# Attention and two mixtures on one core: the first mixture's second product regrouped around what follows it

## The chip, the core and the metric

The kernel runs on one core of a Trainium2 chip. Time is device microseconds (us) of one execution; lower is better. PE (TensorE) multiplies matrices, PEld is its weight loading, DVE (VectorE), ACT (ScalarE) and POOL (GpSimd) work elementwise, and SP (SyncE) issues the DMAs. Each engine works through its own instructions in order and waits for the others by semaphores.

## The reference

Masked attention gives x (2304 tokens by 512). The first mixture multiplies it by `w_in`, bends it, and multiplies by `w_out`; the second reads that result in two places only, in the logits and in the slot inputs.

```
h = x @ w_in                                   # 2304 x 2048
g = where(h >= 1, h, where(h <= -1, 0, (h + 1)**2 / 4))
x2 = g @ w_out                                 # 2304 x 512
logits = x2 @ phi                              # phi: 512 x 32
d = softmax(logits, axis=0)                    # over tokens (dispatch)
slot_input = d.T @ x2                          # 32 x 512, 4 slots for each of 8 experts
slot_out[e] = relu(slot_input[e] @ w1[e]) @ w2[e]
c = softmax(logits, axis=1)                    # over slots (combine)
out = c @ slot_out
```

`w_in` and `w_out` arrive as 64-bit floats and are turned into 32-bit ones on the chip.

## The kernel before

**Attention.** 16 pairs of heads go through a pipeline whose order is written out in `PLAN`. Its steps `xh` and `xl` write x, transposed, as two parts (`xt`): ACT copies the rounded high part out of PSUM, DVE subtracts it to get the low one. In some pairs the plan also prepares a half of a weight tile (`w0` to `w2`): the first `READY` = 4 of 32 tiles are made there.

**Weights.** A tile is 128 by 512 values. `w_raw` loads it by SP (512 KB), `w_mul` scales on ACT, `w_bits` does four DVE operations on the bits (L353 to L356), and `w_parts` makes the high and low part: a copy (ACT in the later part) and two POOL operations (L365, L366). Tiles of `w_in` and `w_out` alternate, and the steps of the last 28 are scattered through the main loop (`prep`).

**Main loop.** The tokens are four blocks of 512 and one of 256 (`BLK`); the hidden features are 16 tiles f of 128. A unit is one block and one f, and `VISITS` sets the order of the 80 units, block after block in turns. `h_unit` makes h with 12 matmuls (4 parts of the inner dimension by three products of high and low parts, L423); ACT, DVE, DVE, ACT and POOL then make g as a high and a low part (L430 to L437). Two units later `out_unit` multiplies: 128 tokens by 512 columns, three matmuls each (L453 to L455), kept in PSUM over a visit and added by DVE into `x2p` at its end (L465).

**Behind the loop.** When a block has all its f, `prework` transposes x2 (L555), multiplies by phi (L564), takes exponentials with a running maximum, and sums x2 by them into S (L600); its steps are let in between matmuls after so many rows (`PACE`). `merge` and `last` do the joining of the four row groups and the 256 tokens, with dummy matmuls (`fill`) in their gaps. The last of it, `p_slots` (L743), writes the slot inputs `st`; `tail` runs the experts on them (L845, L873) and the output. The expert weights, 72 pieces of up to 512 KB, are loaded by `feed` into buffers of 4 KB per partition (pools b4 and c4), as these come free.

PSUM has three pools: ptr (three tiles, for h and small things), psc (two double tiles), ppv (one).

Of the kernel before, what the change touches and what calls it, by code (L numbers as in the profile page):

```python
# [14 lines left out]
P = 128  # L15
# [21 lines left out]
class Pair:  # L37
# [172 lines left out]

    def xl(self, a):
        for hi, lo, src in self.xparts(a):
            self.nc.vector.tensor_tensor(out=lo, in0=src, in1=hi.bitcast(F32), op=ALU.subtract)
# [18 lines left out]
READY = 4  # L232


def attention(e, tc, nb=4, wl=(1, 1 + 2 * READY)):
# [36 lines left out]
    for i, u in fill + plan[len(fill):]:  # L272
        if u[0] != "w":
            pairs[i].step(u)
        else:
# [3 lines left out]
            elif u == "w1":  # L279
                e.moe.w_mul(t, c)  # L280
                for fn in e.moe.w_bits(t, c):
                    fn()
            elif u == "w2":
                for fn in e.moe.w_parts(t, c=c, eng=e.ENG["w"]):
                    fn()


class Moe:


    VISITS = [(0, 0, 2), (1, 0, 2), (2, 0, 3), (3, 0, 4),
# [15 lines left out]


    def b4(self, shape, dt, name):
        return self.e.b4.tile(shape, dt, tag="b4", name=name)  # L310

    def c4(self, shape, dt, name):
        return self.e.c4.tile(shape, dt, tag="c4", name=name)

    def make_xt(self):
        for i in range(4):
            for kk in range(4):
                self.xt[i, kk] = self.b4([P, 2, 512], F32R, f"xt{i}{kk}")
        for u in range(2):
            t = self.b4([P, 2, 2, 256], F32R, f"xt4{u}")  # L320
            for a in range(2):
                self.xt[4, 2 * u + a] = t[:, a]

        def xslice(kk, t):
            i, o = t // 512, t % 512
            x = self.xt[i, kk]
            return (lambda w: x[:, 0, o:o + w]), (lambda w: x[:, 1, o:o + w]), self.BLK[i][1] - o
        self.e.xslice = xslice

# [3 lines left out]
    def w_raw(self, i):  # L333
        e, nc = self.e, self.nc
        f = i // 2
        raw = self.b4([P, 512, 2], U32, f"raw{i}")
        nc.sync.dma_start(raw.rearrange("p c t -> p (c t)"), e.w_out[f * P:(f + 1) * P, :] if i % 2 else e.w_in[f])
        self.wt[i] = raw

    def w_mul(self, i, c=slice(0, 512)):  # L340
        if c.start == 0:
            raw = self.wt[i]
            AB = (self.b4 if i < READY else self.c4)([P, 2, 512], F32, f"wab{i}")
# [4 lines left out]
    def w_bits(self, i, c=slice(0, 512)):  # L348
# [3 lines left out]
        return [  # L352
            lambda: v.tensor_scalar(out=Bu, in0=hi, scalar1=0x80000000, scalar2=None, op0=ALU.bitwise_and),  # L353
            lambda: v.scalar_tensor_tensor(out=Au, in0=Au, scalar=3, in1=Bu, op0=ALU.logical_shift_left, op1=ALU.bitwise_or),  # L354
            lambda: v.tensor_scalar(out=Bu, in0=Au, scalar1=0xff800000, scalar2=None, op0=ALU.bitwise_and),
            lambda: v.scalar_tensor_tensor(out=B, in0=lo, scalar=2.0 ** -52, in1=B, op0=ALU.mult, op1=ALU.mult)]  # L356

    def w_parts(self, i, late=False, c=slice(0, 512), eng="A"):
        p = self.nc.gpsimd
        if c.start == 0:  # L360
# [698 lines left out]
```

## Time and profile before

| | us |
|---|---|
| median of 2 runs | 648.97 (648.87 to 649.07) |
| the profiled execution | 649.23 |
| its span, first to last instruction | 647.4 |
| first h matmul | 174.85 |
| last x matmul gives way to the closing chain | 591.36 |
| first expert matmul | 600.09 |

The profiled execution lies 0.26 us above the median; 1.83 us of its time lie outside the span. The three places of the last rows part it into attention, main loop, closing chain and tail.

### The profile page before, as it was taken

The page shows a single profiled execution, that of the slowest core. Times are in us where ns is not written, and L with a number is a line of the kernel's source. Part 1 is how long each engine was busy: PE and PEld are TensorE (multiplying, and loading weights), DVE is VectorE, ACT ScalarE, POOL GpSimd, SP SyncE. Part 2 cuts the span into 40 slices and gives each one's busy share as a digit, 9 for nine tenths or more (in the row PEclk, how much of TensorE's full clock was granted, in tenths as well). Part 3 has the DMA queues.
Part 4 walks back from the last instruction along what each step waited for, and adds up shares of the span by engine and source line. Part 5 has one row for each costly group of instructions (what it writes and reads, how often), then busy time and mean ns, then how long its engine had stood idle before and what let it go on. Part 6 is the DMA issues. An engine that isn't in the chain of part 4 may idle for free.

```text
span 647.4 us, 11524 instructions
## 1 busy us (share of the span) xinstructions
PE 631.3 (98%) x4351; PEld 499.8 (77%) x4351; DVE 402.7 (62%) x721; ACT 311.1 (48%) x756; POOL 301.4 (47%) x339
## 2 busy tenths in 40 slices
PE   7899999999999999999999999999999999999996
PEld 6777778778788888888888888888888878776355
DVE  6899987877367578756677656647533333444233
ACT  5799999999443444433433333323322232334123
POOL 5798886766235457455465544425622221211000
PEclk8799999999999999999999999999999999999999
DMA  4534324332400031110011120000321344449897
GB/s 130 150 101 143 102 83 116 98 87 60 153 1 32 33 132 65 66 65 1 32 66 66 65 66 33 33 14 33 117 98 66 130 147 147 150 167 340 328 382 293
DMA packets 36086, 71.05 MB, mean 110 GB/s; under 512 B 8000, under 2 KB 17344, under 8 KB 36032
## 3 DMA queue, kind: packets, MB, share of 16 engines
q1 hardware_dynamic: 36032, 70.33, 32.0%
q8 instruction: 34, 0.56, 0.4%
q14 instruction: 20, 0.16, 0.1%
HBM read 64.55 MB, written 4.72 MB: 107 GB/s over the span
## 4 chain that ended last, share of the span: by engine, by line
PE 81%; DVE 9%; ACT 4%; issue 1%; POOL 1%; DVEq 0%; ACTq 0%
PE h L423 28%; PE x L453 10%; PE x L455 10%; PE x L454 10%; PE sc L120 4%; PE om L184 3%; PE eh L845 2%; PE acc L873 2%; DVE nm L142 2%; ACT pr L147 2%; PE ps_1p L166 2%; PE sc L113 1%; PE x2t L555 1%; PE om L189 1%; PE ps_0p L166 1%
## 5 line engine op out<-in xcount | busy, mean ns | idle before, releaser
L423 PE MATMUL h<-xt,w 128*128 128x512 f32 (+1 forms) x960 | 212.6, 369 | 0.0
L437 POOL TENSOR_TENSOR g<-ga,g 128x512 fp32r<-128x512 f32 (+1 forms) x80 | 98.6, 1232 | 226.5 <-ACT g L436 197.2
L423 PEld LDWEIGHTS h<-xt,w 128*128 128x128 f32 x960 | 168.5, 188 | 32.5 <-issue 1.8
L432 DVE SCALAR_TENSOR_TENSOR ga<-ga 128x512 f32<-128x512 f32 (+1 forms) x80 | 70.0, 875 | 148.9 <-ACT ga L430 148.8
L453 PE MATMUL x<-w,g 128*128 128x512 f32 x288 | 115.0, 399 | 1.5 <-ACT x2p L241 0.7
L436 ACT CAST g<-ga 128x512 fp32r<-128x512 f32 (+1 forms) x80 | 46.3, 579 | 139.3 <-DVE ga L434 139.3
L454 PE MATMUL x<-w,g 128*128 128x512 f32 x288 | 112.3, 390 | 0.0
L455 PE MATMUL x<-w,g 128*128 128x512 f32 x288 | 112.3, 390 | 0.0
L430 ACT ACTIVATE ga<-h,half 128x512 f32<-128x512 f32 (+1 forms) x80 | 51.6, 645 | 107.2 <-PE h L423 100.5
L158 POOL TENSOR_SCALAR pr<-pr,sm 128x384 f32<-128x384 f32 (+2 forms) x144 | 85.4, 613 | 24.4 <-ACT Q L89 11.4
L147 ACT ACTIVATE pr<-sc,nm 128x512 f32<-128x512 f32 (+2 forms) x144 | 78.6, 559 | 6.4 <-DVE nm L140 3.8
L453 PEld LDWEIGHTS x<-w,g 128*128 128x128 f32 x288 | 54.1, 188 | 16.9 <-issue 3.6
L455 PEld LDWEIGHTS x<-w,g 128*128 128x128 f32 x288 | 54.1, 188 | 11.5
L454 PEld LDWEIGHTS x<-w,g 128*128 128x128 f32 x288 | 54.2, 188 | 9.8
L142 DVE TENSOR_REDUCE nm<-sc 128x2 f32<-128x1024 f32 (+1 forms) x64 | 52.3, 818 | 5.4 <-PE sc L123 4.0
L434 DVE TENSOR_TENSOR ga<-h,ga 128x512 f32<-128x512 f32 (+1 forms) x80 | 50.7, 634 | 1.9
L120 PE MATMUL sc<-K,Q 64*128 64x512 f32 (+3 forms) x384 | 47.7, 364 | 2.7 <-ACT pr L147 2.7
L365 POOL TENSOR_TENSOR wab<-wab,w 128x512 f32<-128x512 f32 (+1 forms) x36 | 44.6, 1238 | 11.6 <-ACT w L241 6.8
L366 POOL TENSOR_TENSOR w<-wab 128x512 fp32r<-128x512 f32 (+1 forms) x36 | 44.5, 1237 | 1.9
L120 PEld LDWEIGHTS sc<-K,Q 64*128 64x128 f32 x384 | 30.5, 198 | 12.3 <-ACT pr L147 4.9
L465 DVE TENSOR_TENSOR x2p<-x,x2p 128x1024 f32<-128x1024 f32 (+1 forms) x32 | 36.8, 1181 | 0.6 <-PE x L455 0.4
L354 DVE SCALAR_TENSOR_TENSOR wab<-wab 128x512 uint32<-128x512 uint32 (+1 forms) x36 | 32.4, 901 | 1.4
(202 smaller groups left out, 774.2 us busy)
## 6 DMA issues: line engine op xcount, KB each, us to landing
ew<-in_w_dram SPq DMA_DIRECT2D x32, 512.0 KB, 4.5
raw<-in_w_in_dram SPq DMA_DIRECT2D x16, 512.0 KB, 3.3
raw<-in_w_out_dram SPq DMA_DIRECT2D x16, 512.0 KB, 3.3
ew<-in_w2a_dram SPq DMA_DIRECT2D x16, 510.0 KB, 6.6
ew<-in_w2b_dram SPq DMA_DIRECT2D x16, 344.0 KB, 6.9
kn<-in_k_dram SPq DMA_DIRECT2D x16, 288.0 KB, 3.7
qn<-in_q_dram SPq DMA_DIRECT2D x16, 288.0 KB, 3.2
vn<-in_v_dram SPq DMA_DIRECT2D x16, 256.0 KB, 3.2
```

Source lines behind the costliest of these rows:

```text
L120: nc.tensor.matmul(sc[:, h, 0:n], self.Q[r, qa, 128 * i:128 * i + 128], self.K[r, ka, 0:n], start=(k == 0), stop=False)
L142: nc.vector.tensor_reduce(out=self.negm[:, 2 * i:2 * i + 2], in_=self.scs[i][:, :, 0:128 * (i + 1)], axis=AX.X, op=ALU.max, negate=True)
L147: self.nc.scalar.activation(pr, sc, AF.Exp, bias=self.negm[:, b:b + 1], accum_out=self.sums[:, b:b + 1])
L158: self.nc.gpsimd.tensor_scalar(out=pr, in0=pr, scalar1=self.sums[:, b:b + 1], scalar2=1.0, op0=ALU.mult, op1=ALU.mult)
L423: nc.tensor.matmul(ph[:, 0:n], w[:, wi, kk], x[:, xi, 0:n], start=(m == 0), stop=(m == 11))
L430: nc.scalar.activation(ga, ph, AF.Relu, bias=e.half[:, 0:1], scale=0.5)
L432: nc.vector.scalar_tensor_tensor(out=ga, in0=ga, scalar=1.0, in1=ga, op0=ALU.min, op1=ALU.mult)
L434: nc.vector.tensor_tensor(out=ga, in0=ph, in1=ga, op=ALU.max)
L437: nc.gpsimd.tensor_tensor(out=gl, in0=ga, in1=gh.bitcast(F32), op=ALU.subtract)
L453: nc.tensor.matmul(px, gh[:, c], w[:, 0], start=first, stop=False)
L454: nc.tensor.matmul(px, gh[:, c], w[:, 1], start=False, stop=False)
L455: nc.tensor.matmul(px, gl[:, c], w[:, 0], start=False, stop=last)
```

## The change

x2 is no longer formed. The logits are g times (`w_out` times phi), and the slot inputs are (dispatch sums of g) times `w_out`. In parts:

- `w_out` tiles are made by one POOL addition, stored to DRAM (`wod`) by SP, and loaded again as `wo` in units 42 to 49. `wo_turn` transposes them, `wo_phi` multiplies by phi, `wo_back` turns the product into `w2p` (128 by 32 for each f).
- All `w_in` tiles come first (i below 16), then `w_out`. `READY` is 6. The unit order is plainly block 0 with all 16 f, block 1, and so on; one tile is prepared in each of the units 0 to 25, as `run` writes it out.
- g is one 32-bit tile, written by DVE at L520. `act_unit` uses three ACT operations and one DVE operation in units 0 to 27, one ACT and two DVE after that. The POOL subtraction of g is gone.
- `quad(b, q)` takes four f of a block: it transposes g (L534; ACT copies the result), and multiplies `w2p` by g into the logits, which stay in the ppv tile over the block (L540). `soft`, `disp` and `weigh` are the former softmax steps. `slots` sums the transposed g by the dispatch weights, 2048 columns wide, where S had 512.
- `sides` writes by unit number what stands behind each unit; `PACE`, `VISITS` and `tick` go.
- `chain` follows the last unit: the last quad, the softmax of the 256 tokens, their slots, then `turn` (S transposed and weighted), `inputs` (times `wo`) and `spread` (into `st`). It has no dummy matmuls.
- In blocks 2 to 4 attention writes x once, by DVE; `split` makes the two parts in the loop (ACT and POOL).
- Buffers are taken and given back by count (`new`, `drop`; 47 in all), and `feed` asks `room`, which goes through the plan of a dry run.

```diff
-            self.nc.scalar.copy(hi, src)
+            if lo is None:
+                self.nc.vector.tensor_copy(hi, src)
+            else:
+                self.nc.scalar.copy(hi, src)
...
-READY = 4
+READY = 6
...
+        if i >= 16:
+            p.tensor_tensor(out=A, in0=A, in1=B, op=ALU.add)
+            self.nc.sync.dma_start(self.e.wod[:, i - 16], A)
+            return
...
+        for kk in range(4):
+            nc.tensor.transpose(ps[:, kk], A[:, kk * P:(kk + 1) * P], e.ident)
+        e.copy("A", self.wT[f // 2][:, f % 2], ps)
...
+                nc.tensor.matmul(ps[32 * i:32 * i + 32, 0:P], e.phi[:, kk], self.wT[2 * c + i // 2][:, i % 2, kk],
+                                 start=(kk == 0), stop=(kk == 3))
...
+        nc.tensor.transpose(ps[:, 0:P], self.wp, e.ident)
+        nc.vector.tensor_copy(e.w2p[:, 4 * c:4 * c + 4].rearrange("p i s -> p (i s)"), ps[:, 0:P])
...
-        nc.scalar.copy(gh, ga)
-        nc.gpsimd.tensor_tensor(out=gl, in0=ga, in1=gh.bitcast(F32), op=ALU.subtract)
...
-            nc.tensor.matmul(px, gh[:, c], w[:, 0], start=first, stop=False)
-            nc.tensor.matmul(px, gh[:, c], w[:, 1], start=False, stop=False)
-            nc.tensor.matmul(px, gl[:, c], w[:, 0], start=False, stop=last)
...
+        if on == "A":
+            nc.scalar.activation(ga, ph, AF.Relu, bias=e.half[:, 0:1], scale=-0.5)
+            nc.scalar.activation(ga, ga, AF.Relu, bias=e.unit[:, 0:1], scale=-1.0)
+            nc.scalar.activation(ga, ga, AF.Square)
+        else:
+            nc.scalar.activation(ga, ph, AF.Relu, bias=e.half[:, 0:1], scale=0.5)
+            nc.vector.scalar_tensor_tensor(out=ga, in0=ga, scalar=1.0, in1=ga, op0=ALU.min, op1=ALU.mult)
+        nc.vector.tensor_tensor(out=g, in0=ph, in1=ga, op=ALU.max)
...
+                    nc.tensor.transpose(ps[:, a, i * P:(i + 1) * P], self.gt(b, f)[:, o:o + P], e.ident)
...
+                nc.tensor.matmul(self.lt[32 * j:32 * j + 32, 0:P], e.w2p[:, f], self.gt(b, f)[:, j * P:(j + 1) * P],
+                                 start=(f == 0), stop=(f == 15))
...
+            e.copy("A", t, self.gn[b, q, u])
...
+                nc.tensor.matmul(ps[32 * j:32 * j + 32, a], v["en"][:, 32 * j:32 * j + 32],
+                                 self.gn[b, 2 * r + a, j // 2][:, j % 2], start=True, stop=True)
...
+            nc.vector.scalar_tensor_tensor(out=S, in0=S, scalar=v["f"], in1=ps[0:R], op0=ALU.mult, op1=ALU.add)
...
+            nc.tensor.matmul(ps[:, i], self.S[r][:, i // 4, i % 4 * P:(i % 4 + 1) * P], self.selw, start=True, stop=True)
...
+            nc.tensor.matmul(self.si[g:g + 32], self.sg[:, f], self.wo[f // 2][:, f % 2], start=(f < 4), stop=(f > 11))
...
+            e.copy("AD"[k0 // 2], s4[:, c], self.si[:, c])
+            ps = e.ptr.tile([P, 2, 32], F32, tag="tr", name=f"t_i{k0}")
+            for k in range(2):
+                nc.tensor.matmul(ps[:, k], s4[:, (k0 + k) * P:(k0 + k + 1) * P], e.sel4[:, 0:32], start=True, stop=True)
...
+        first = 16 - READY
+        for f in range(16):
+            k = put(first + f + 3, "wo_turn", f)
+            if f % 4 == 3:
+                put(k + 2, "wo_phi", f // 4)
+                back = put(k + 3, "wo_back", f // 4)
+                free = put(max(back + 1, f + 2), "quad", 0, f // 4)
+        for b in range(4):
+            put(free, "soft", b)
+            put(free + 1, "disp", b)
+            put(free + 2, "slots", b, 0)
+            put(free + 3, "slots", b, 1)
+            put(free + 4, "weigh", b)
+            if b < 3:
+                for q in range(4):
+                    free = put(max(free + 1, 16 * b + 16 + 4 * q + 5), "quad", b + 1, q)
+        for q in range(3):
+            put(64 + 4 * q + 6, "quad", 4, q)
+        for b in range(2, 5):
+            for u, fn in enumerate(self.split(b)):
+                put(16 * b - (4 if b == 2 else 6) + u, fn)
+        for u in range(8):
+            put(42 + u, "wo_load", u)
...
+            if READY < i <= 32:
+                self.w_parts(i - 1)
+            if i < 32:
+                self.w_bits(i)
+                if i + 1 < 32:
+                    self.w_mul(i + 1)
+                if i + 2 < 32:
+                    self.w_raw(i + 2)
+            self.h_unit(b, f)
+            self.act_unit(b, f, "A" if i < 34 else "D")
+            for fn, *a in at.get(k, []):
+                (getattr(self, fn) if isinstance(fn, str) else fn)(*a)
...
+        for step in (lambda: self.quad(4, 3), lambda: self.soft(4), self.maximum, lambda: self.disp(4), lambda: self.comb(0),
+                     self.weights, lambda: self.slots(4, 0), lambda: self.slots(4, 1), lambda: self.comb(1),
+                     lambda: self.turn(0), lambda: self.turn(1), lambda: self.inputs(0), lambda: self.inputs(1), self.spread):
```

On PE, in the main loop, this stood before, at the end of one unit's x and the start of the next unit's h:

```order
L453 MATMUL x_1121_5211<-w_4857,g_14_5241 128x512
L454 MATMUL x_1121_5211<-w_4857,g_14_5241 128x512
L455 MATMUL x_1121_5211<-w_4857,g_14_5241 128x512
L423 MATMUL h_13_5332<-xt_150,w_4534 128x512 x3
L423 MATMUL h_13_5332<-xt_151,w_4534 128x512 x3
L423 MATMUL h_13_5332<-xt_152,w_4534 128x512 x3
L423 MATMUL h_13_5332<-xt_153,w_4534 128x512 x3
```

Now, behind unit 20, PE has the second half of a quad, one turn of a `w_out` tile (wt), and the next h:

```order
L534 MATMUL gn_3529<-ident,g_0_2856 128x128 x2
L534 MATMUL gn_3529<-ident,g_2_2917 128x128 x2
L540 MATMUL lt_3538<-g_0_2856,w2p 32x128 x8
L540 MATMUL lt_3538<-g_2_2917,w2p 32x128 x8
L460 MATMUL wt_3559<-ident,wab_3335 128x128 x4
L501 MATMUL h_5_3575<-xt_144,w_1916 128x512 x3
L501 MATMUL h_5_3575<-xt_145,w_1916 128x512 x3
```

The x matmuls are gone; transposes and logits of four f stand together between two units.

On DVE, in the early main loop before (wab is a weight tile in work, ga the g in work):

```order
L432 SCALAR_TENSOR_TENSOR ga_0_2957<-ga_0_2957 128x512
L354 SCALAR_TENSOR_TENSOR wab_2869<-wab_2869 128x512
L434 TENSOR_TENSOR ga_0_2957<-h_0_2943,ga_0_2957 128x512
L355 TENSOR_SCALAR wab_2869<-wab_2869 128x512
L356 SCALAR_TENSOR_TENSOR wab_2869<-raw_2836,wab_2869 128x512
L432 SCALAR_TENSOR_TENSOR ga_1_2996<-ga_1_2996 128x512
L434 TENSOR_TENSOR ga_1_2996<-h_1_2982,ga_1_2996 128x512
```

Now, in unit 2:

```order
L428 TENSOR_SCALAR wab_2870<-raw_2841 128x512
L429 SCALAR_TENSOR_TENSOR wab_2870<-wab_2870 128x512
L430 TENSOR_SCALAR wab_2870<-wab_2870 128x512
L431 SCALAR_TENSOR_TENSOR wab_2870<-raw_2841,wab_2870 128x512
L520 TENSOR_TENSOR g_2_2917<-h_2_2904,ga_2_2918 128x512
L428 TENSOR_SCALAR wab_2900<-raw_2872 128x512
```

The four bit operations of a tile stand in one run in each unit, ahead of the unit's g, where they were scattered.

On PE, from the last sums over tokens (sl) to the first expert matmul (eh) before; ct is the combine weights turned:

```order
L731 MATMUL sl<-x2p_3440,EL 32x512 x2
L820 MATMUL x_1241_5950<-identr,n_5971 128x128 x4
L743 MATMUL t_s_6164<-sel_124,S 128x32 x2
L743 MATMUL t_s_6169<-sel_124,S 128x32 x2
L845 MATMUL eh_6182<-ew_5044,st 32x512 x2
```

And now, from the joint maximum (t_m) on; s are the sums over tokens, si the slot inputs:

```order
L622 MATMUL t_m<-ident,nm 1x128
L577 MATMUL et_5712<-ident,E_5696 128x64
L820 MATMUL ct_5716<-identr,n_5458 128x128 x4
L631 MATMUL t_b<-ones,row 128x2
L587 MATMUL s_5729<-gn_5453,en_5714 32x512 x2
L587 MATMUL s_5729<-gn_5558,en_5714 32x512 x2
L587 MATMUL s_5739<-gn_5652,en_5714 32x512 x2
L587 MATMUL s_5739<-gn_5693,en_5714 32x512 x2
L820 MATMUL ct_5749<-identr,n_5463 128x128 x4
L658 MATMUL t_s_5755<-selw,S_4160 128x32 x8
L658 MATMUL t_s_5767<-selw,S_4226 128x32 x8
L668 MATMUL si<-wo_4562,sg 32x512 x2
```

Between the sums and the experts there are now 16 matmuls of turning and 16 of multiplying by `wo` (and spreading, behind these rows).

## Rows read from the trace of the kernel before

**Rows 1.** Windows: per engine, busy us (count); then granted clock, DMA share, GB/s.
```profile
5.00:10.00 5.00, 2.77 (x25) 1.93 (x22) 3.47 (x5) 2.51 (x8) 1.40 (x1) 0.99 0.55 176
10.00:15.00 5.00, 4.03 (x24) 3.42 (x26) 4.03 (x10) 3.87 (x13) 4.78 (x7) 0.50 0.11 41
...
100.00:140.00 40.00, 40.00 (x440) 32.25 (x439) 30.37 (x69) 38.11 (x118) 27.82 (x42) 1.00 0.37 103
...
175.00:592.00 417.00, 415.47 (x2061) 339.08 (x2062) 244.81 (x351) 145.27 (x260) 176.49 (x141) 1.00 0.22 77
...
600.00:648.00 48.00, 42.01 (x482) 22.25 (x481) 14.83 (x41) 11.62 (x29) 0.69 (x2) 0.97 0.85 334
```

**Rows 2.** Timeline of PE, first h and a pure stretch: start, length, line, tiles, count.
```profile
174.85 8.50 PE L423 MATMUL h<-xt,w 128*128 128x512 f32 x36
...
511.64 2.88 PE L423 MATMUL h<-xt,w 128*128 128x512 f32 x12
514.36 0.39 PE L453 MATMUL x<-w,g 128*128 128x512 f32 x1
...
517.08 2.21 PE L423 MATMUL h<-xt,w 128*128 128x512 f32 x9
```

**Rows 3.** Timeline of PE among the steps behind a block.
```profile
565.36 0.60 PE L555 MATMUL x2t<-ident,x2p 128*128 128x128 f32 x4
565.72 0.48 PE L453 MATMUL x<-w,g 128*128 128x512 f32 x1
...
567.73 0.64 PE L564 MATMUL lt<-x2T,phi 128*32 128x128 f32 x16
568.30 1.70 PE L423 MATMUL h<-xt,w 128*128 128x256 f32 x12
569.84 0.27 PE L592 MATMUL et<-ident,E 128*128 128x128 f32 x1
...
571.42 1.07 PE L600 MATMUL s<-x2p,en 128*32 128x512 f32 x8
572.41 0.50 PE L453 MATMUL x<-w,g 128*128 128x512 f32 x1
```

**Rows 4.** Timeline of PE, closing chain and first experts.
```profile
591.36 1.09 PE L684 MATMUL x2tl<-ident,x2p 128*128 128x128 f32 x8
...
599.08 1.08 PE L743 MATMUL t_s<-sel,S 64*128 64x32 f32 x8 [0.21 <-DVE S L735]
600.09 7.07 PE L845 MATMUL eh<-ew,st 128*32 128x512 f32 x64
```

**Rows 5.** Weight steps by line: ns min/median/max, and when.
```profile
L353 DVE TENSOR_SCALAR wab<-raw x28: 408/416/797, 180.1 to 453.7; 128x512 uint32<-128x512 uint32 x28
L354 DVE SCALAR_TENSOR_TENSOR wab<-wab x28: 676/690/1783, 180.6 to 457.0; 128x512 uint32<-128x512 uint32 x28
L355 DVE TENSOR_SCALAR wab<-wab x28: 409/427/1508, 181.3 to 457.7; 128x512 uint32<-128x512 uint32 x28
L356 DVE SCALAR_TENSOR_TENSOR wab<-raw,wab x28: 674/682/1772, 183.2 to 462.4; 128x512 f32<-128x512 uint32 x28
L365 POOL TENSOR_TENSOR wab<-wab,w x28: 1272/1292/1757, 195.6 to 465.6; 128x512 f32<-128x512 f32 x28
```

**Rows 6.** Timeline: a POOL and a DVE operation that meet.
```profile
195.60 1.29 POOL L365 TENSOR_TENSOR wab<-wab,w 128x512 f32<-128x512 f32 x1 [2.41 <-ACT w L241]
...
195.66 1.78 DVE L354 SCALAR_TENSOR_TENSOR wab<-wab 128x512 uint32<-128x512 uint32 x1
```

**Rows 7.** DVE by line and form from 180 us: busy us, mean ns, idle.
```profile
L434 DVE TENSOR_TENSOR ga<-h,ga 128x512 f32<-128x512 f32 x64 | 44.0, 687 | 1.5
```

**Rows 8.** ACT by line and form from 180 us.
```profile
L430 ACT ACTIVATE ga<-h,half 128x512 f32<-128x512 f32 x63 | 43.3, 688 | 90.5 <-PE h L423 85.2 <-POOL g L437 3.1 <-POOL wab L365 2.3
...
L346 ACT ACTIVATE wab<-raw 128x512 f32<-128x512 f32 x27 | 17.9, 664 | 0.0
...
L241 ACT COPY x2p<-x 128x1024 f32<-128x1024 f32 x5 | 5.0, 1007 | 0.0
```

More of the change, by code (lines that the diff above doesn't have):

```diff
@@ L312, in c4 @@
-    def c4(self, shape, dt, name):
-        return self.e.c4.tile(shape, dt, tag="c4", name=name)
-    def make_xt(self):
[L316 to L322, printed above, removed]
+        self.dry = live is not None
+        self.live = dict(live or {"b4": 0, "c4": self.CAP["c4"]})
@@ new lines, in drop, with room @@
+    def drop(self, *names):
+        for name in names:
+            self.live[self.home.pop(name)] -= 1
+            self.tape.append(-1)
+    any4 = new
+    def room(self, key):
+        at = len(self.tape)
+        held = [self.ends[k] for k in self.ew if self.ends[k] >= at] + [self.ends[key]]
+        base = sum(self.live.values()) - len(held) + 1
+        gone = sorted(held)
+        if base + len(held) > self.cap:
+            return False
+        k = 0
+        for t in range(at, len(self.plan)):
+            x = self.plan[t]
+            if x in (1, -1):
+                base += x
+            while k < len(gone) and gone[k] <= t:
+                k += 1
+            if base + len(gone) - k > self.cap:
+                return False
+        return True
@@ new lines, in xslice, with split, one @@
+            return (lambda w: x[:, o:o + w]), None, room
+        self.e.xslice = xslice
+    def split(self, i):
+        n = self.BLK[i][1]
+        for u in range(n // 256):
+            def one(u=u):
+                hi, lo = self.xt[i, u] = [self.new([P, 1024 // n, n], F32R, f"x{c}{i}{u}") for c in "hl"]
+                self.nc.scalar.copy(hi, self.xw[i, u])
+                self.nc.gpsimd.tensor_tensor(out=lo, in0=self.xw[i, u], in1=hi.bitcast(F32), op=ALU.subtract)
+                self.drop(f"xw{i}{u}")
+            yield one
@@ L351, in w_bits @@
         Au, Bu = A.bitcast(U32), B.bitcast(U32)
[L352 to L356, printed above, removed]
@@ L368, in w_work @@
-    def w_work(self):
-        raw = lambda i: [lambda: self.w_raw(i)] if i < 32 else []
-        mul = lambda i: [lambda: self.w_mul(i)] if i < 32 else []
-        bits = lambda i: self.w_bits(i) if i < 32 else []
-        yield from raw(READY) + raw(READY + 1) + mul(READY)
-        for i in range(READY, 33):
-            parts = []
-            if i > READY:
-                while i - 1 >= self.done + self.WIN:
-                    yield None
-                parts = self.w_parts(i - 1, late=self.w_pool(i - 1) == "c4")
-            b = bits(i)
-            for k in range(4):
-                yield from b[k:k + 1] + parts[k:k + 1]
-            yield from raw(i + 2) + mul(i + 1)
-        self.free["b4"] += 2
-        self.free["c4"] += 3
@@ L388 @@
-    LULL = 2, 3
-    def prep(self, n):
-        for _ in range(0 if self.k in self.LULL else n):
-            step = next(self.work, None)
-            if step is None:
-                return
-            step()
-    WIN = 12
-    PACE = ((4000, 2000, 0, 0, 4500, 1900, 5100, 2300, 1000),
[3 rows of a table removed]
-    def tick(self, rows):
-        if len(self.side) > self.keep:
-            self.credit += rows
-            if self.credit >= self.side[0][0]:
-                self.credit -= self.side[0][0]
-                self.side.pop(0)[1]()
-                self.feed()
```

641 lines of the change are left out of this document (297 added, 344 removed), and 6 rows, old and new, of tables (PACE, VISITS).

## The prediction

> **What bounds the kernel now.** I read the windows first, one stretch of the program at a time. In the main loop TensorE is busy 415.47 of 417 us at a granted clock of 1.00, while DVE has 244.8, ACT 145.3 and POOL 176.5 us of work, and the DMA engines are used for .22 of the time [rows 1]. So in that stretch only work taken off TensorE counts. The timeline of TensorE prices that work. An h of 512 tokens starts at 511.64 and the next x at 514.36: 2.72 us for 12 matmuls, .227 each. From there to the next h it is again 2.72 us for 12 x matmuls [rows 2]. Three marks part the execution: attention until the first h at 174.85 [rows 2], the loop until 591.36 (416.5 us), the closing chain until the first expert matmul at 600.09 (8.73 us) [rows 4], and the tail until 647.4 (47.3 us). In the tail the DMA engines are the busiest thing, .85 and 334 GB/s [rows 1]. The profiled execution took 649.23 us, .26 over the median, with 1.83 us outside its span; I sum against 649.23 and leave both as they are. A measurement of this kernel can tell some 2%, or 13 us, from no change.
>
> **TensorE's work in the loop.** What goes: 18 token groups by 16 f by 3 = 864 x matmuls at .227, 196 us, together with the x2 transposes and narrow logits behind each block. What is there afterwards:
> - h as before: 64 units at 2.72 = 174.1, and 16 units of 256 tokens at 1.54 (568.30 to 569.84 [rows 3]) = 24.6.
> - Transposes of g and `w_out`: 288 + 64 = 352. Four took .36 us (565.36 to 565.72 [rows 3]), so .09 each, 31.7.
> - Logits: 8 matmuls of 128 columns took .57 (567.73 to 568.30 [rows 3]), .071 each with four row groups side by side. 256 for blocks 0 to 3 = 18.2; 32 for block 4, which fills only two groups, at twice that = 4.6; 64 of `wo_phi` = 4.6.
> - Slots of blocks 0 to 3: 64 matmuls of 512 columns, four together in .99 (571.42 to 572.41 [rows 3]) = 15.9.
> - Small ones 1; the last quad, 1.9, belongs to the chain.
>
> That is 273 us, 143 less than now. It is the lower bound of the loop.
>
> **Where TensorE will have to wait.** With h alone a unit is 2.72 us long where it was 5.44, so the other engines' work per unit, which was free, is now to be held against it.
>
> Units 1 to 10 prepare a `w_in` tile each. DVE's four bit operations take .416, .690, .427 and .682, and POOL's two take 1.29 each [rows 5]. They don't run side by side freely: L354 has a longest of 1.783 and L356 of 1.772 [rows 5], and the timeline shows one of them, started at 195.66 within a POOL operation that ran 195.60 to 196.89, ending .55 us after it [rows 6]. It stood still while POOL worked. If the three operations that stretch (1.80 us together) and POOL's 2.58 exclude each other, a unit takes 4.37 us. The max of g (.687 [rows 7]) reads PSUM and L353 starts from raw; I count both as covered. ACT has less: .66 for `w_mul`, .69 out of PSUM, and two more of .66 [rows 8], with the tile's copy 3.3. So 4.37 sets the pace, 1.65 more than TensorE's 2.72: ten times, **+16.5**. The bounds are 0 (the tiles made ahead and three PSUM tiles let TensorE run on) and 5.49 a unit if nothing overlaps at all, .42 + 1.80 + 2.58 + .69, +28. Units 11 and 12 drop one POOL operation: +2.
>
> Units 13 to 25: TensorE has 2.72, a turn of .36 and its part of quads and `wo_phi`, 3.73 on average. ACT has .66 + .69 + 2 × .66 in the unit, .69 for the turned tile, and per quad two copies of 1024 columns at 1.007 [rows 8], .50 a unit: 3.86. DVE has 2.9 and a part of POOL's single 1.29. SP is new in this circle: it stores each `w_out` tile when POOL has added it, and that wait stands ahead of the next raw load, which `w_mul` waits for, and then the bits. Each link is short, but they close a ring over two units. I take 4.1 a unit: 13 × .37 = **+5**, with 0 and +18 (5.1 a unit) as ends.
>
> After that: 16 quads and 8 slot steps share two double PSUM tiles, which ACT or DVE must empty at about 1.0 per 1024 columns [rows 8] while they also have g to make. A matmul of the next step finds the tile taken for part of that; I take half a copy each time, 24 × .5 = **+12**. None of it if the steps are far enough apart, 24 if whole copies show. The moved `split` (ACT and POOL, a few units) and `wo_load` (eight loads of stored tiles, at a DMA share of .22 [rows 1]) I cost at nothing, since h keeps TensorE busy over them; if that cover is gone they are at most 1.3 us a unit in ten units, inside the ends already named.
>
> Loop: 273 + 16.5 + 2 + 5 + 12 = **308.5**, between 273 and about 345. Against 416.5 that is −108.
>
> **The chain.** It now carries more on the path: turn, 16 matmuls of the kind that took 1.01 per four (599.08 to 600.09 [rows 4]), 4.0; inputs, 16 at .99 per four, 4.0; spread, 1.0; slots of the 256 tokens, 8 in pairs at .99 [rows 3], 4.0; the last quad 1.9. That is 14.9. The waits between: the last g (ACT .69, DVE twice .69 [rows 7, 8]), and five copies or sums of some 1.0 between the products, 7. So 22 us against 8.7, **+13**; 15 if all waits hide, 28 if they are double.
>
> **Attention and tail.** `READY` 6 adds two tiles there: 4.4 us of DVE and 5.2 of POOL [rows 5]; in blocks 2 to 4 one part of x goes. In 100 to 140 us TensorE is busy 40.0 of 40, DVE 30.4, POOL 27.8, ACT 38.1 [rows 1], so there is room and nothing to gain: 0, with −2 and +4. The tail does the same work on the same bytes: 0.
>
> Sum: 649.23 − 108 + 13 = 554.2, and with the roundings I say **555 us**.
>
> **Rivals.** (1) *The ring tightens.* If preparation has no overlap at all, a unit takes the 5.49 us above in all of units 0 to 25: 143 us where the forecast has about 108. +35, **590** (575 to 605). For it: DVE runs the four bit operations in one row ahead of the unit's max, so a late raw tile holds back the max, the PSUM tile of h and then TensorE, and 47 buffers with nearly none to spare couple the loads to what is given back. Against: six tiles are ready, a lead of five units.
>
> (2) *TensorE alone sets the loop.* The lead of the tiles made ahead covers the early units and the exclusion of DVE and POOL is as mild as the medians say [rows 5]. Then the 23.5 us of units 1 to 25 go: **531** (515 to 541). For it: medians stand next to their minima, .690 against .676. Against: POOL now meets the bit operations in every unit.
>
> (3) *The expert weights come late.* Some 35 pieces, 17.7 MB, have to land between unit 63 and the first expert, some 60 us by my own sum: 295 GB/s, where the tail shows 334 [rows 1]. At three quarters of that they take 71 us: +10, **565**.
>
> (4) *Slower: the clock.* At 5 to 10 us TensorE was busy 2.77 of 5 and in the next 5 us its granted clock was .50, the 1.2 GHz level [rows 1]. The new loop has gaps and crowds of transposes, and the new chain has no dummy matmuls. Each us of TensorE's work done at half clock adds one; from 94 of the 273 us on the change costs more than it brings, and with all of them the time is **828**. Against: from 100 to 140, where attention also turns its probabilities on TensorE between matmuls, the clock is 1.00 [rows 1], and a loop that waits 35 us of 308 is still busy for .89. The Trainium skill ("TensorE: Matmul & The Clock Gate", Part 4: PE-mode transpose) says that full clock doesn't engage for transposes, which don't count as a busy engine. By that rule quads would pull the clock down and the time would go towards rival 4's; the row of 100 to 140 speaks against it, but its transposes stand thinner than a quad's sixteen.
>
> That the x matmuls stay in some form is excluded: the order of instructions holds none, and their number is known.
>
> **Chances.** The forecast, 555 with 541 to 575 around it, .50; rival 1 .22, rival 2 .19, rival 3 .05, rival 4 .04. The range runs from 525, which leaves out the lower third of rival 2, to 594, which leaves out the upper third of rival 1 and rival 4: 525 to 594. Faster by over 2% is everything but rival 4 and a little of its neighbourhood: .93; within 2%, a clock lost for half that stretch, .03; slower .04.
>
> **What the next profile should show.** The max of g at L520 every 4.4 us in units 1 to 10, with L429 and L431 stretched by POOL L446 and L447 ahead of it; 5.5 there would be rival 1, 2.7 rival 2. The stretch from first h to the last one's quad 308 us, TensorE busy about .89 of it at clock 1.00; h still 2.72. The first expert matmul (L844) 22 us behind it and the tail 47 us long; a longer tail with DMA idle before it is rival 3. A granted clock near .5 behind a quad would be rival 4. I'm wrong if preparation paces units 13 to 25 too (5 us and more), if PSUM tiles make every quad wait a whole copy, or if attention ends later than 179.

## The result and the profile after

The changed kernel takes 563.62 us (561.42 to 565.82) where the first took 648.97: a ratio of 0.8685, with an interval of 0.8539 to 0.8831. It is faster by about 85 us, inside the range and 8.6 us above the forecast of 555. The profiled execution took 561.42 us with a span of 559.6.

The same three marks part it. The timeline of TensorE gives the first h, and two units further on:

```profile
178.92 13.94 PE L501 MATMUL h<-xt,w 128*128 128x512 f32 x60
194.18 3.02 PE L501 MATMUL h<-xt,w 128*128 128x512 f32 x12 [1.33 <-DVE g L520]
198.50 3.02 PE L501 MATMUL h<-xt,w 128*128 128x512 f32 x12 [1.29 <-DVE g L520]
```

The 60 matmuls at the start are five units in a row; from then on a unit takes 4.32 us (194.18 to 198.50). (In the counts of these views some matmuls stand as two: the x16 of s below are 8 of the program, and the x32 of t_s and si are 16.) The closing chain, again in the timeline of TensorE:

```profile
488.94 0.49 PE L534 MATMUL gn<-ident,g 128*128 128x128 f32 x3
490.59 0.77 PE L534 MATMUL gn<-ident,g 128*128 128x128 f32 x5 [1.16 <-DVE g L520]
...
493.99 0.27 PE L622 MATMUL t_m<-ident,nm 128*1 128x128 f32 x1 [1.64 <-DVE nm L570]
...
495.27 5.32 PE L587 MATMUL s<-gn,en 128*32 128x512 f32 x16
500.53 0.54 PE L820 MATMUL ct<-identr,n 128*128 128x128 f32 x4
500.90 3.72 PE L658 MATMUL t_s<-selw,S 128*128 128x32 f32 x32
504.56 3.64 PE L668 MATMUL si<-wo,sg 128*32 128x512 f32 x32
...
510.73 3.64 PE L844 MATMUL eh<-ew,st 128*32 128x512 f32 x32
```

The last quad starts at 488.94, the first expert matmul at 510.73. Put beside the forecast:

| | before | forecast | after |
|---|---|---|---|
| attention, to the first h | 174.85 | 174.85 | 178.92 |
| loop, to the last quad | 416.5 | 308.5 | 310.0 |
| chain, to the first expert matmul | 8.73 | 22 | 21.8 |
| tail, to the end of the span | 47.3 | 47.3 | 48.9 |

The windows of the same execution (columns as in [rows 1]; the last two are one quad and a piece of the chain):

```profile
100.00:140.00 40.00, 38.26 (x421) 30.27 (x421) 35.05 (x78) 34.03 (x104) 32.64 (x48) 1.00 0.38 105
178.92:240.00 61.08, 48.03 (x202) 36.03 (x200) 55.59 (x72) 42.79 (x68) 33.79 (x24) 1.00 0.38 136
240.00:300.00 60.00, 50.44 (x396) 40.42 (x397) 37.95 (x67) 43.86 (x69) 15.88 (x13) 1.00 0.43 146
300.00:400.00 100.00, 99.03 (x830) 76.50 (x832) 41.94 (x69) 41.06 (x59) 10.77 (x6) 1.00 0.16 54
400.00:488.90 88.90, 88.76 (x719) 72.31 (x709) 42.47 (x87) 32.03 (x56) 4.12 (x4) 1.00 0.42 150
...
383.90:386.70 2.80, 2.80 (x49) 2.46 (x47) 1.59 (x3) 2.38 (x3) 0.00 (x0) 1.00 0.13 48
496.00:498.00 2.00, 2.00 (x8) 0.57 (x6) 0.14 (x1) 0.00 (x0) 0.00 (x0) 0.50 0.00 0
```

TensorE still bounds the loop from 300 us on (99.03 of 100 and 88.76 of 88.9 us busy), but not the first 120 us of it: 48.03 of 61 and 50.44 of 60. From 178.92 to 240 DVE is busy 55.59 of 61.08. What TensorE waits for in the loop, by the view of waits (total us, times, longest):

```profile
PE h L501 <- DVE g L520: 12.9, 10, 1.3
PE wt L460 <- ACT wT L246: 4.1, 4, 1.7
PE wt L460 <- ACT gn L246: 3.3, 2, 1.9
PE wback L478 <- DVE wp L473: 2.3, 1, 2.3
PE gn L534 <- DVE S L592: 1.0, 2, 0.5
```

23.6 us in all, 12.9 of them for the max of g in the early units, and next to nothing after block 0's quads. This view counts from the modelled end of the last matmul. By the starts, a unit that waits for the max is 4.31 − 2.72 = 1.59 longer than one in a row of h, where the view shows 1.29; ten of them are 15.9, and all waits together some 27.

### The profile page after: what moved, and what is told of

It is laid out like the page before. It is cut to its first block, busy times and chain, and to the rows that moved or that the text cites. A ratio compares the mean times of both kernels' runs of the same rounds, so it can differ in the third digit from the quotient of the medians.

```text
span 559.6 us, 11650 instructions
## 1 busy us (share of the span) xinstructions
PE 511.5 (91%) x4492; PEld 387.9 (69%) x4492; DVE 344.2 (62%) x679; ACT 319.9 (57%) x723; POOL 196.7 (35%) x255
## 4 chain that ended last, share of the span: by engine, by line
PE 55%; DVE 22%; ACT 10%; issue 4%; DMA 3%; POOL 2%; SPq 0%; DVEq 0%; POOLq 0%; ACTq 0%
PE h L501 25%; PE gn L534 5%; ACT pr L147 5%; DVE wab L429 4%; DVE nm L142 3%; PE lt L540 3%; PE s L587 3%; DMA raw<-in_w_out_dram 3%; PE om L184 3%; PE eh L844 3%; PE acc L871 2%; DVE wab L428 2%; DVE PT L248 2%; DVE g L520 2%; DVE sm L152 1%
## 5 line engine op out<-in xcount | busy, mean ns | idle before, releaser
L501 PE MATMUL h<-xh,w 128*128 128x512 f32 (+1 forms) x384 | 108.9, 362 | 0.0
L501 PE MATMUL h<-xt,w 128*128 128x512 f32 x384 | 95.0, 398 | 13.0 <-DVE g L520 12.9
L501 PEld LDWEIGHTS h<-xt,w 128*128 128x128 f32 x384 | 70.0, 188 | 31.5 <-DVE g L520 17.4
L519 DVE SCALAR_TENSOR_TENSOR ga<-ga 128x512 f32<-128x512 f32 (+1 forms) x52 | 34.2, 658 | 93.6 <-ACT ga L518 93.6
L501 PEld LDWEIGHTS h<-xh,w 128*128 128x128 f32 x384 | 68.5, 189 | 18.4 <-issue 8.0
L501 PE MATMUL h<-xl,w 128*128 128x512 f32 (+1 forms) x192 | 68.2, 355 | 0.0
L520 DVE TENSOR_TENSOR g<-h,ga 128x512 f32<-128x512 f32 (+1 forms) x80 | 51.0, 637 | 27.9 <-ACT ga L516 25.3
L120 PE MATMUL sc<-K,Q 64*128 64x512 f32 (+3 forms) x384 | 47.2, 360 | 3.6 <-ACT pr L147 2.8
L246 ACT COPY gn<-gn 128x1024 f32<-128x1024 f32 x36 | 35.2, 1012 | 11.9 <-PE gn L534 10.5
L120 PEld LDWEIGHTS sc<-K,Q 64*128 64x128 f32 x384 | 29.8, 193 | 14.0 <-ACT pr L147 7.2
L501 PEld LDWEIGHTS h<-xl,w 128*128 128x128 f32 x192 | 36.3, 189 | 4.5
L534 PE MATMUL gn<-ident,g 128*128 128x128 f32 x288 | 35.5, 274 | 2.1 <-DVE g L520 1.2
L534 PEld LDWEIGHTS gn<-ident,g 128*128 128x128 f32 x288 | 32.1, 140 | 6.3 <-issue 1.7
L446 POOL TENSOR_TENSOR wab<-wab,w 128x256 f32<-128x256 f32 (+1 forms) x22 | 24.9, 1132 | 25.7 <-PE h L501 13.1
L422 ACT ACTIVATE wab<-raw 128x512 f32<-128x512 f32 (+1 forms) x38 | 22.7, 599 | 19.1 <-DMA raw<-in_w_out_dram 11.9
```

The lines of the kernel that those rows point to most:

```text
L120: nc.tensor.matmul(sc[:, h, 0:n], self.Q[r, qa, 128 * i:128 * i + 128], self.K[r, ka, 0:n], start=(k == 0), stop=False)
L246: nc.scalar.copy(dst, src)
L446: p.tensor_tensor(out=A, in0=A, in1=w[:, 0].bitcast(F32), op=ALU.subtract)
L501: nc.tensor.matmul(ph[:, 0:n], w[:, wi, kk], self.x(b, kk, xi)[:, 0:n], start=(m == 0), stop=(m == 11))
L519: nc.vector.scalar_tensor_tensor(out=ga, in0=ga, scalar=1.0, in1=ga, op0=ALU.min, op1=ALU.mult)
L520: nc.vector.tensor_tensor(out=g, in0=ph, in1=ga, op=ALU.max)
```

## The experiments

Every run is compared with the first kernel on the same chip; the changed kernel stands there at 563.43 (561.41 to 565.49) when it is run again. "Unit by unit" means the starts of the max of g on DVE, one for each of the 80 units.

**The changed kernel again.** 

> The changed kernel once more, as the ground for the others. Attention to 179, first h to last quad 310, chain 22, tail 49, total 561 to 566.

 Ratio 0.8682 (0.8659 to 0.8706). In its profile the loop is 312.4 and the chain 23.2: unit by unit its units 0 to 18 lie within .2 us of the first profile, 2.3 us are lost between units 18 and 25, and 1.4 in the chain. Both go with the granted clock, which was 1.00 through the loop of the first profile and is .94 here from 240 to 300 us: two h behind waits of 2.4 and 2.0 us take 4.5 instead of 3.0, and in the chain the 16 matmuls with `wo` take 5.3 instead of 3.6.

```profile
261.60 4.52 PE L501 MATMUL h<-xt,w 128*128 128x512 f32 x12
```

So differences of 2 us in these two places say nothing by themselves. The first h scatters too, from 178.61 to 179.86 in the eight profiles whose attention is the same, but most of this arises in the first 45 us. From the 96th of the 384 score matmuls of L120 to the first h these eight take 133.6 to 134.2, the first kernel 128.7, so attention is read by that stretch below. The tail lies between 47.8 and 50.9 in the thirteen profiles of the changed kernel and its variants.

**One POOL operation less.**

```diff
+        if eng == "A":
+            p.tensor_tensor(out=w[:, 1], in0=A, in1=w[:, 0].bitcast(F32), op=ALU.subtract)
+        else:
         p.tensor_tensor(out=A, in0=A, in1=w[:, 0].bitcast(F32), op=ALU.subtract)
         p.tensor_tensor(out=w[:, 1], in0=A, in1=B, op=ALU.add)
```

> Leaves out one of the two POOL operations on each w_in tile prepared in the main loop (the low part is A minus the high part, without B), nothing else. Theory (DVE stands still while POOL works): the unit of the stretch 194 to 229 falls from 4.31 by POOL's 1.36 to about 2.9 to 3.1, and the execution by 10 to 13 us. Rival (DVE's own operations, ACT or TensorE set 4.31): under 2 us.

 Measured: 553.38 us, 0.8538 (0.8522 to 0.8554), 10 less. Unit by unit the pace is 3.34, and 9.7 us are won between unit 0 and unit 10 (the first h came .3 earlier); .4 of it is lost again by unit 28. The timeline of the changed kernel, units 5 and 6 (start, length, engine, line, operation), shows the mechanism:

```profile
206.00 1.58 POOL L446 TENSOR_TENSOR wab<-wab,w 128x512 f32<-128x512 f32 x1 [1.28 <-ACT w L246]
206.37 0.68 DVE L520 TENSOR_TENSOR g<-h,ga 128x512 f32<-128x512 f32 x1
...
206.97 0.90 DVE L428 TENSOR_SCALAR wab<-raw 128x512 uint32<-128x512 uint32 x1
...
207.66 1.36 POOL L447 TENSOR_TENSOR w<-wab 128x512 fp32r<-128x512 f32 x1
...
207.90 1.67 DVE L429 SCALAR_TENSOR_TENSOR wab<-wab 128x512 uint32<-128x512 uint32 x1
209.61 0.62 ACT L246 CAST w<-wab 128x512 fp32r<-128x512 f32 x1 [1.09 <-DVE wab L429]
209.61 0.43 DVE L430 TENSOR_SCALAR wab<-wab 128x512 uint32<-128x512 uint32 x1
210.07 0.69 DVE L431 SCALAR_TENSOR_TENSOR wab<-raw,wab 128x512 f32<-128x512 uint32 x1
...
210.68 0.68 DVE L520 TENSOR_TENSOR g<-h,ga 128x512 f32<-128x512 f32 x1
```

DVE has no gap: max .68, first bit operation .90, second 1.67, then .43 and .69. The second one starts at 207.90, while POOL works from 206.00 to 209.02, and ends .55 after POOL, as in [rows 6]. It is stretched from .69 to 1.67, the first one from .42 to .90. The max, which reads PSUM, is not, nor is the last bit operation. With one POOL operation:

```profile
205.16 0.91 DVE L428 TENSOR_SCALAR wab<-raw 128x512 uint32<-128x512 uint32 x1
...
206.11 0.69 DVE L429 SCALAR_TENSOR_TENSOR wab<-wab 128x512 uint32<-128x512 uint32 x1
...
207.53 1.60 POOL L447 TENSOR_TENSOR w<-wab,w 128x512 fp32r<-128x512 f32 x1 [1.74 <-ACT w L246]
```

The second bit operation is back at .69, the first still at .91. So the rival (DVE's own operations, ACT or TensorE set the pace) falls. The saving is .97 a unit and not POOL's whole 1.36, since the one taken out began (207.66) beside the first bit operation and held up the second only from 207.90 on.

**POOL's work one unit later.**

```diff
-            if READY < i <= 32:
+            if READY + 1 < i <= 17:
+                self.w_parts(i - 2)
+            if 16 < i <= 32:
                 self.w_parts(i - 1)
```

> ACT's copy and POOL's two operations on a w_in tile come one unit later, so that they never wait for the bit operations of the same unit; no work is left out. Theory that only the exclusion of DVE and POOL sets the pace: 1.80 + 2.58 still have to go one after the other, 4.3 a unit, 0 us. Rival, a ring (bit operation, copy, two POOL operations, next bit operation): the pace falls to 3.0 to 3.4, total 7 to 10 us less.

 Measured: 564.08 us, 0.8711 (0.8683 to 0.8738), the pace 4.31 as before. But the run doesn't decide between the two, for the edit parts the engines for a few tiles only. Its timeline, first while it does, then in the steady state:

```profile
191.76 1.34 POOL L447 TENSOR_TENSOR w<-wab 128x512 fp32r<-128x512 f32 x1
...
192.00 1.65 DVE L431 SCALAR_TENSOR_TENSOR wab<-raw,wab 128x512 f32<-128x512 uint32 x1
...
203.71 1.67 DVE L429 SCALAR_TENSOR_TENSOR wab<-wab 128x512 uint32<-128x512 uint32 x1
...
205.42 0.62 ACT L246 CAST w<-wab 128x512 fp32r<-128x512 f32 x1 [0.35 <-DVE wab L429]
```

In unit 2 POOL's operations follow each other, all four bit operations of the tile are held up (1.33, 1.67, 1.41, 1.65), and the unit takes 6.69. From the next one on ACT, which now runs further ahead, waits with its copy for the second bit operation of the same tile again (205.38, copy at 205.42), as it does in the changed kernel (209.57, 209.61). So a ring is there, and its links add up to the pace: copy .62, POOL 1.59 and 1.36, .55 from POOL's end to the end of the next tile's second bit operation, and gaps of .19, together 4.31. That DVE stands still while POOL works is the link that closes it. Whether the exclusion would set the same pace without the copy in the ring wasn't tried.

**Dummy matmuls early and late.**

```diff
+        if 16 * b + f in (4, 5, 6, 7, 8, 9, 48, 50, 51, 52, 54, 55):
+            self.fill(ph[:, 0:P], 14)
```

> 14 dummy matmuls of 128 columns (.06 to .07 each, 0.9 us) ahead of h in units 4 to 9 and in six units between 48 and 55. Theory: in units 4 to 9 TensorE waits 1.29 for the max, so the six cost 0 to 1 us together and the pace stays 4.31; in the late units they cost their full length, 5 to 6 us. Rival, that TensorE sets both: about 11. Rival, that neither counts: 0.

 Measured: 565.81 us, 0.8721 (0.8706 to 0.8735). The timeline of TensorE in the early units (L833 are the dummies):

```profile
198.50 0.94 PE L833 MATMUL h<-warm 128*128 128x128 bf16 x14 [0.57 <-DVE g L522]
199.25 3.00 PE L503 MATMUL h<-xt,w 128*128 128x512 f32 x12
```

They take .75 each time and the pace stays 4.31; unit by unit the early six change nothing (0.00 to −0.03 us). The late six cost 4.9 us, from the max of unit 47 to that of unit 55: 37.13 where it was 32.26. (The time is only 2.4 longer, since units 11 to 25 came out 1.3 shorter in this profile, and by the scatter named above.) TensorE has room in the one stretch and none in the other.

**Transposes among the h matmuls.**

```diff
+                for t in mix:
+                    for _ in range(2 if m < 5 else 1):
+                        next(t, None)
```

(`mix` issues the transposes of a quad; the quad keeps its logits and copies behind h.) 

> Only the order on TensorE: the transposes of g (16 of a quad in 1.84 us, .115 each) are issued one or two at a time between the 12 h matmuls of the same unit. Theory that a transpose costs what loading 128 by 128 weights takes, and that this can hide under one 512-wide matmul but not under a 128-wide one: .10 to .12 each again, loop within 4 us of 311. Rival, that a fixed gap around a row of transposes makes the price: .055 each, loop 16 us shorter.

 Measured: 575.65 us, 0.8875 (0.8858 to 0.8891), 12 more. In the pure stretch the price is what the theory says. In the changed kernel a quad reads:

```profile
383.88 1.92 PE L534 MATMUL gn<-ident,g 128*128 128x128 f32 x16
385.72 1.08 PE L540 MATMUL lt<-g,w2p 128*32 128x128 f32 x32
386.73 0.50 PE L501 MATMUL h<-xh,w 128*128 128x512 f32 x1
387.07 0.40 PE L501 MATMUL h<-xl,w 128*128 128x512 f32 x1
```

16 transposes in 1.84 (383.88 to 385.72), .115 each. Mixed, one h matmul and one transpose take .34 together (398.62 to 398.96), .113 over the .227 of h alone:

```profile
398.62 0.27 PE L537 MATMUL gn<-ident,g 128*128 128x128 f32 x1
398.64 0.48 PE L501 MATMUL h<-xl,w 128*128 128x512 f32 x1
398.96 0.27 PE L537 MATMUL gn<-ident,g 128*128 128x128 f32 x1
```

A quad's unit there comes to within .15 us of the old one. That the weight load is the reason fits, but only the price was measured. The loss is elsewhere: unit by unit it comes in steps of 4.8, 4.3, 3.8 and 2.2 us at units 20, 24, 28 and 32, those with the quads of block 0, and none behind. The view of waits names transposes that wait 5.7 us for ACT's copies of turned tiles (wT): a PSUM tile is still held, and now part of an h stands behind it. By the starts the loop's waits come to 38 where they were 27, which is 11 of the 14 us that the loop lost. The rest goes with the granted clock, .91 from 240 to 300 us in this profile. The expectation of "within 4 us" missed that.

**The closing chain filled.**

```diff
+        self.fill(self.gap, 18)
...
+    lambda: self.soft(4), lambda: self.fill(self.gap, 24), self.maximum,
```

> The closing chain with 18 dummy matmuls ahead of the last quad and 24 behind its logits, no other change. Theory that the two waits there lower the granted clock to .50 at 496 to 498: with the clock kept at 1.00 the 8 slot matmuls take 4.0 instead of 5.26 and the chain is 1 to 1.5 us shorter. Rival, that the chain's elementwise steps set its length: unchanged or longer by up to 1.

 Measured: 561.49 us, 0.8658 (0.8639 to 0.8676), an interval that overlaps the changed kernel's. In the profile the 8 slot matmuls take 3.55 (5.26 without the dummies), the clock is 1.00 throughout, and the first expert starts 20.1 us after the last h. But several runs with no dummies in the chain (four tiles, the later copy, POOL's store, below) have the same 3.6 and 20.1 to 20.4. And with the dummies, in the run of READY 9 below, the clock fell all the same:

```profile
490.00:493.00 3.00, 3.00 (x28) 2.54 (x24) 1.40 (x2) 0.72 (x2) 0.00 (x0) 1.00 0.63 172
493.00:496.00 3.00, 3.00 (x18) 2.46 (x21) 0.42 (x1) 0.24 (x1) 0.00 (x0) 0.59 0.92 360
496.00:500.00 4.00, 4.00 (x24) 0.98 (x20) 0.00 (x0) 0.00 (x0) 0.00 (x0) 0.50 0.74 201
```

At 490 to 493 TensorE is busy 3.00 of 3.00, then the granted clock is .59 and .50; the 16 matmuls with `wo` take 6.1 instead of 3.64. So this stays open: in some of the profiled executions the chain loses 1.7 to 3.5 us to the half clock, in others nothing. It fell in seven of the ten profiles without dummies and in one of the three with them, so the dummies aren't shown to prevent it.

**Four tiles in attention.**

```diff
-def attention(e, tc, nb=4, wl=(1, 1 + 2 * READY)):
+def attention(e, tc, nb=4, wl=(1, 1 + 2 * 4)):
...
+        for i in (4, 5):
+            self.w[i] = self.w[i - 4]
```

> Two of the six weight tiles made in attention are left out (units that need tiles 4 and 5 use 0 and 1), so attention prepares four as before and the loop is unchanged. Theory that the two tiles cost attention its 4 us: first h at 175, total 4 us less. Rival, that the single x write in blocks 2 to 4 costs it: first h stays at 179.

 Measured: 561.56 us, 0.8665 (0.8643 to 0.8688); first h at 178.15, 0.9 less than in the run again. From the 96th score matmul on attention takes 132.3, 1.3 to 1.8 less than in the eight profiles with six tiles. So the two tiles are some 1.6 of what attention lost there (5.2, from 128.7 to some 133.9), under a third, and the theory that they are all of it falls.

**The x copy later on DVE.**

```diff
     def xh(self, a):
         for hi, lo, src in self.xparts(a):
-            if lo is None:
-                self.nc.vector.tensor_copy(hi, src)
-            else:
+            if lo is not None:
                 self.nc.scalar.copy(hi, src)
     def xl(self, a):
         for hi, lo, src in self.xparts(a):
             if lo is None:
+                self.nc.vector.tensor_copy(hi, src)
                 continue
```

> In attention the one copy of x in blocks 2 to 4 is moved on DVE from the earlier step xh to the later xl; same engine, same work. Theory that at xh DVE stands waiting for TensorE's om (9.1 us in seven waits) with the row maxima queued behind it, and that this costs attention its 4 us: first h at 175 to 176.5, total 2 to 4 us less. Rival, that more DVE and POOL work there costs it: first h stays at 178 to 179.

 Measured: 558.51 us, 0.861 (0.8591 to 0.863), 5 less; first h at 176.51. The waits of DVE in attention, of the changed kernel and then of this run:

```profile
DVE xw L210 <- PE om L189: 9.1, 7, 4.3
```

```profile
DVE xw L215 <- PE om L189: 5.0, 2, 2.9
```

The same copy waits 9.1 us for TensorE in the one place and 5.0 in the other. At the earlier place the row maxima stand behind it on DVE. From the 96th score matmul on attention takes 130.6, 3.0 to 3.5 less than in the eight profiles. So the place of the copy is some 3.3 of the 5.2 us, and with the two tiles' 1.6 all but some .3 is found, if the two add. The rest of the 5 us isn't attention's: in this profile the chain kept its clock and took 20.1.

**Two more tiles made ahead.** The diff is one line, `READY = 8`. 

> READY 8 in place of 6, all else by the same rules. Theory: two units less at 4.31 us where TensorE needs 2.72, so the loop is 2.5 to 3.2 us shorter, and attention 0.8 longer (as the run without two tiles says): total 2 us less, 561 to 562. Rival, that the tiles cost attention 2 us each: no gain or worse.

 Measured: 558.63 us, 0.8619 (0.86 to 0.8638), 4.8 less than the changed kernel. First h 180.81; from the 96th score matmul on attention takes 134.8, .8 more, as expected. The loop is 306.1, and the waits for the max of g fall from 12.8 to 10.3. The whole is more than expected: the loop is 3.9 shorter than in the first profile of the changed kernel instead of 2.5 to 3.2, and the tail is 1.1 shorter, both within the scatter.

**The store issued by POOL.**

```diff
-            self.nc.sync.dma_start(self.e.wod[:, i - 16], A)
+            p.dma_start(self.e.wod[:, i - 16], A)
```

> The store of a finished w_out tile is issued by POOL in place of SP, so it no longer stands ahead of the next raw load. Theory of the prediction (this store closes the ring that makes TensorE wait in units 11 to 25, about 10 us in all): those waits fall by 3 us or more. Rival, that ACT's queue (scaling, three steps of g, copies of turned tiles) holds TensorE there: the waits and the total unchanged within 1 us.

 Measured: 557.98 us, 0.8603 (0.8589 to 0.8617), 5.5 less. The loop is 306.1. Between 230 and 300 us ACT's scaling waits 3.8 us for raw tiles where it was 11.9, and TensorE's waits in the loop are:

```profile
PE h L501 <- DVE g L520: 11.6, 9, 1.3
PE wback L478 <- DVE wp L473: 3.8, 1, 3.8
PE wt L460 <- ACT gn L246: 1.0, 2, 0.6
PE gn L534 <- DVE S L592: 1.0, 2, 0.5
```

17.4 in place of 23.6. Unit by unit the gain is 4.0 us and lies in units 12 to 25. So the store in SP's queue, which waits for POOL and holds up the next raw load, was some 4 of the 9.7 us that TensorE waited there. The view's waits fell by more, 6.2; part of that is lost again where the granted clock drops behind the wait of 3.8 (to .54, 258 to 261). The chain, which kept its clock in this profile, is 1.7 more.

**Together.** Best8 has the later copy, the dummies and READY 8; best9 has READY 9. 

> Three edits at once: the x copy later on DVE in attention, the dummy matmuls of the closing chain, READY 8. If they add, 2.4 to 4.9 + 1.5 to 2 + 2 us less than the changed kernel: 555 to 557, ratio to the first kernel .857. Rival, that they meet (the later copy needs the DVE time that two more tiles take): 558 or more.

 

> The same with READY 9. By the theory one more unit at 2.72 in place of 4.31, less 0.4 in attention: 1.2 us below best8. Rival, that the ninth tile is finished too late in attention, behind its last pairs: the first h comes 2 us later and the gain is gone.

 Measured: 553.43 us, 0.8538 (0.8521 to 0.8555), and 553.57, 0.8539 (0.8512 to 0.8566). Both beat the changed kernel by 10 us, which is a little more than was expected, and the ninth tile brings nothing measurable (its profile holds the clock's fall above). First h is at 176.04 and 176.39: with the later copy, the extra tiles cost attention little (131.1 and 131.3 from the 96th score matmul on, where the later copy alone has 130.6). POOL's store wasn't tried with them.

## Why the prediction held, step by step

**TensorE's work in the loop, 273: too small by 10.** The loop of 310.0 less some 27 of waiting, by the starts, is 283. The price of a transpose in a long row was mis-sized: .115 and not .09, and for the 288 of the quads that is 7.2. I had divided a row of four by four, from its start to the start of the next x [rows 3]; but that x starts .03 behind the last transpose and is late itself (565.72 to 566.03, .31 where an x takes .227). The 16 turns, rows of four, took the .35 that I had for them, with a late h behind. These changes from one kind to another had no term: the first h behind a quad's logits takes .34 (386.73 to 387.07) instead of .227, about 4 us for 40 changes (16 quads, 8 slot steps, 16 turns). Logits were a little cheaper, 16 in 1.01, some 3 us less in all.

**Units 1 to 10, +16.5: right in the link, near in size, in part by luck.** 4.37 a unit was forecast and 4.31 measured, and that a bit operation stands still while POOL works is what makes the unit long (one operation less: 3.34). But the sum behind 4.37, 1.80 of DVE and 2.58 of POOL, is not what runs: the ring holds ACT's copy, which I had as free (.62), POOL's two at 2.95, and .55 of DVE. What I counted as covered was not quite that either: the first bit operation is stretched too, while part of POOL's work lies beside the max. By the starts TensorE lost 15.9 in ten waits, close to the 16.5. That it had run five units ahead only moved them, to units 5 to 14. So rival 2 (the lead hides it) didn't come, and neither did rival 1 (5.49 a unit).

**Units 11 to 25, +7: 9.7 measured** (4.1 + 3.3 + 2.3 in the waits). The ring over SP's store was named, and the run with POOL's store shows it to be some 4 of them. What is left there the waits put down to copies by DVE and ACT; two of them (3.3, for gn) are turns that find a PSUM tile not yet emptied of a quad, the kind of wait that I had looked for later on.

**Waits for PSUM tiles later, +12: wrong.** 1.0 us in two waits. 16 quads and 8 slot steps hardly ever meet a taken tile, a copy of 1.0 being done while an h takes 2.72. This error and that of TensorE's work, in opposite directions, are why the loop came out within 1.5 us. That is luck.

**Chain, +13: 21.8 for 22**, but from other pieces. The work was priced a little high (turn 3.66 and inputs 3.6 for 4.0 each). The waits that the timeline names come to 4.2 (1.16 and 1.64 above, .49 and .87 ahead of the two spreads), not 7. And 1.7 us are the clock: between 496 and 498 it is .50, the slot matmuls take 5.26, and in undisturbed runs 3.6. That is rival 4 in small. In the loop of this profile the clock stays at 1.00, through a quad's sixteen transposes as well (383.90 to 386.70); in nine of the twelve other profiles it falls between 240 and 300 us, where TensorE still waits (means of .91 to .98), and in the run again that cost the loop 2.4. From 300 to 480 it is 1.00 in all. So the Trainium skill's remark that full clock doesn't engage for transposes ("TensorE: Matmul & The Clock Gate", Part 4: PE-mode transpose) is not what a quad's row shows, 1.84 us long between h matmuls; no run has a longer row. The stretch that went to half clock held matmuls, behind two waits.

**Attention, 0: wrong, +4.1** at the first h, at the end of the bound, and beyond it from the 96th score matmul on, where it is 5.2 (128.7 to 133.9); the first 45 us came out 1.1 shorter (45.0 for 46.2; 44.6 to 46.0 in all thirteen profiles). I read DVE's 30.4 of 40 us as room [rows 1]. The busy share doesn't tell what stands in the queue: the copy waits for TensorE in front of row maxima that TensorE needs soon. Now TensorE is busy 38.26 of 40 there. Some 3.3 us are shown to be the place of the copy and some 1.6 the two tiles, which the forecast had at nothing; that TensorE waits for just those maxima is argued.

**Tail, 0: +1.6.** What the DMA engines moved in the tail, first of the kernel before, then after:

```profile
DMA packets 5635, 16.03 MB, mean 334 GB/s; under 512 B 628, under 2 KB 756, under 8 KB 5630
```

```profile
DMA packets 6648, 19.19 MB, mean 384 GB/s; under 512 B 744, under 2 KB 872, under 8 KB 6644
```

19.19 MB in place of 16.03: more of the expert weights came inside the tail, the engines had hardly a gap left, and the stores of the output landed later: 6.3 us after their issue for the first six where it was 5.0, and the last five are issued 8.0 us before the end of the span (551.56) where it was 6.7 (640.75). That is rival 3 in small, 1.6 us where it had 10. It is read from the two traces and wasn't tried, and the size is uncertain by the tail's scatter (47.8 to 50.9 behind the change; only one profile stands before it).

The sum from the measured pieces: 649.23 + 4.1 − 106.5 + 13.1 + 1.6 = 561.5, against 561.42.

## What to carry to other kernels

When a bound engine loses half its work, write down for each stretch what every other engine does per unit, and look for the pair that can't work side by side; the pace could then be had from rows of the old trace to within 2%, though not from the right links: follow the ring of waits too. A short row of matmuls is to be priced from its neighbours' starts as well: here the x behind the row paid part of it (.31 for .227). Busy shares say whether an engine has time, not whether its queue is in the right order: an instruction that gets a new engine needs a new place in that engine's order.

## What the hardware showed that I had not expected

- Beside POOL, the operation on DVE that reads PSUM (the max, .68) ran at its usual length. Two that began while POOL worked, on SBUF alone, ended .29 and .55 behind POOL's operation, .90 long instead of .42 and 1.67 instead of .69. The last bit operation, begun .24 before POOL's, kept its .69, and POOL's took 1.58 to 1.61 instead of 1.29.
- A 128 by 128 transpose takes .113 to .115 us between h matmuls of 512 columns just as in a long row of its own kind.
- The granted clock fell to .50 for a few us in the chain of eight of the thirteen profiles, and in nine of them in the loop between 240 and 300 us, behind waits of 2.0 us (the run again) to 3.8 (POOL's store). The same waits stood in other profiles without a fall, and in one chain it fell when TensorE had been busy without a gap for 3 us. Between the changed kernel's two profiles this is where the 4 us of difference lie.
